# Re-ordered queues in an RWKV-7 recurrence with a SwiGLU feed-forward on one core

## The chip, the cores and the metric

The kernel runs on one core of a Trainium2 chip. The metric is the device time of one launch in microseconds (us). A core has five engines that run side by side, each with a queue of its own that it works off in order: TensorE (PE in the profile, its weight loads PEld), VectorE (DVE), ScalarE (ACT), GpSimd (POOL) and SyncE (SP). SP only issues transfers (DMAs). POOL also issues transfers, and ACT a few at the start. An engine whose next instruction waits for a semaphore holds up all that stand behind it in its queue.

## The reference

`B, H, S, D` are 4, 8, 768 and 40. First comes a recurrence over the tokens, for 32 sequences with a 40x40 state each, then a feed-forward over 3072 tokens with a model width of 320 and a hidden width of 1536:

```python
for t in range(S):
    y[:, :, t] = einsum('bhd,bhde->bhe', r[t], state)
    Sa = einsum('bhde,bhe->bhd', state, a[t])
    state = state * w[t][:, :, None, :] - einsum('bhd,bhe->bhde', Sa, b[t]) + einsum('bhd,bhe->bhde', v[t], k[t])
x = y.transpose(0, 2, 1, 3).reshape(B * S, H * D)
xn = x / sqrt(mean(x * x, -1) + 1e-6) * rms_g
out = (silu(xn @ w_gate) * (xn @ w_val)) @ w_out          # all float32
```

## The kernel before, in words

The recurrence is cut into 24 chunks of 32 tokens. A chunk `c` goes through three stages.

- `front(c)` (lines 652 to 758) loads the inputs of the chunk, turns them with TensorE (`turned`, tiles `wan`, `kbn`), and multiplies up the decays level by level (tiles `T`, `A`, `Ab`, `K`, `KN`). At each level TensorE forms products (`gramk`, `ps<-Ab,K` in the profile), VectorE picks parts of them out of PSUM into the triangular matrix `LT` (COPY_PREDICATED, `where`), and ScalarE copies others (`KN<-ps`, `K<-K`). At its end `LT` goes by DRAM (`sB`) into a layout for the inversion, tile `M`.
- `inverse(c)` (lines 760 to 776) inverts that matrix on VectorE with 31 pairs of dependent steps, `tmp<-Yi,M` and `Yi<-Yi,tmp`, and sends the result by DRAM (`sY`) back into `LT`. For the first four chunks `early_inverse(c)` (lines 778 to 806) does half of it on VectorE within `M` and the rest with small matmuls on TensorE (`ps<-M,LT`, `ps<-M`).
- `main(c)` (lines 810 to 937) carries the state: `ps<-ST,aP` and `ps<-VU,LT` give the right-hand side `Xs`, `ps<-Xs,LT` (early: `ps<-Xs,M`) solves it, copies put the solution into `VU` (line 830), `ps<-VU,KN` updates the state `ST`. Then come scores, masked by VectorE and ScalarE into `As` (lines 864 to 876), the level products `ps<-As,KN` summed on VectorE into `y`, the turn of `y`, the norm (`ss`, `x`), and `xg`, the turned input of the feed-forward.

After each pair of chunks `feed(g)` (lines 939 to 970) runs the feed-forward of 256 tokens: for 12 slices of the hidden width the matmuls `ps<-xg,wf` (kinds `h64` and `h`), a SiLU on ScalarE (`sg`, line 962), a product on VectorE (`hT`), and `po<-wf,hT` into the accumulator `po`. The weights of a slice are loaded from DRAM tensors `sW` into one of five buffers `wf`. The tensors `sW` are made once, during the first third, by `narrow` (lines 973 to 991): it loads raw weights into a `wf` buffer, reworks them in three ScalarE and three VectorE steps (`ex`), and stores them.

None of this is issued in the order in which it is written. The helpers (`tt`, `copy`, `act`, `dma`, `pe` and so on, lines 442 to 495) only record pieces. A piece is one instruction, or one group of matmuls of TensorE. `Plan.issue` (lines 322 to 350) then emits the 6028 pieces in the order of the string `ORDER` (lines 33 to 226): each number is a piece, counted from the first piece not yet issued, and each `-` is a filler, a matmul of the identity with itself into an unused part of `po` (line 1015, `po<-ident` in the profile; two instructions), which gives TensorE something to do. So `ORDER` fixes the queue of every engine. The second string, `PAIRS` (lines 228 to 234), tells for each of the 499 uses of PSUM which of three two-bank tiles (`ps0` to `ps2`) it takes; a use can only begin when the one before it on that tile has been read.

Of the kernel before, what the change touches and what calls it, by code (L numbers as in the profile page):

```python
# [33 lines left out]
85 84 76 83 58 78 73 86 74 59 60 75 5 89 61 88 53 77 80 4 43 6 201 7 87 90 44 8 334 62 9 - - - - - - - - 93 10 18 79  # L34
11 12 214 557 13 213 567 14 15 94 566 210 16 17 95 558 108 200 - - - 97 96 19 335 20 21 2 209 22 23 98 25 199 568 26
100 578 202 24 101 107 569 111 57 - - - - - 102 106 124 589 27 122 112 392 109 103 52 119 113 104 54 577 155 125 110
204 105 120 - - - - - - 114 203 117 121 559 211 598 118 46 131 129 132 45 562 560 212 597 563 588 561 394 123 115 136
586 384 133 134 - - - - - 126 130 116 47 564 3 145 383 135 336 128 137 48 144 143 141 587 219 142 51 570 127 565 146
138 337 55 573 1005 216 579 281 393 220 582 608 571 390 234 379 239 607 572 583 580 380 251 574 222 38 221 609 575 581
42 - - - - - - - - 223 82 226 339 91 64 227 338 39 81 139 224 263 576 238 153 56 249 247 590 206 584 228 382 237 591  # L40
272 593 40 233 232 585 381 154 148 594 33 140 205 229 592 389 235 250 28 248 - - 325 236 32 245 36 230 147 260 282 391
246 259 150 35 34 326 595 0 36 270 155 214 148 242 243 62 605 598 230 - 239 40 616 599 601 628 64 49 91 600 602 30 48
626 1135 28 257 603 29 241 68 150 255 65 0 1347 194 0 194 84 173 0 - - - 182 540 200 0 557 184 1 186 935 542 540 0 506
515 527 257 513 300 0 111 97 110 61 112 96 51 439 458 122 50 243 480 0 244 0 58 255 242 0 259 709 104 120 246 708 247
456 470 258 488 719 0 256 470 457 242 0 716 265 487 104 0 268 0 0 265 473 0 262 277 0 273 0 236 0 260 0 269 0 461 241
- - - - - - - 237 242 0 0 278 242 243 252 0 252 0 0 89 0 99 246 0 97 0 230 94 440 0 230 94 440 231 - - - - - - - - -
240 441 244 0 0 468 440 451 255 0 42 468 269 469 258 215 440 239 204 0 0 257 253 203 93 449 92 212 0 235 - - - - - - -
- 246 0 437 0 262 0 246 247 436 245 464 470 258 259 469 260 244 - - 255 471 465 468 466 0 215 466 269 256 445 697 255
478 686 93 94 264 95 687 270 96 266 97 0 97 470 695 2 98 99 3 100 471 101 473 1 102 0 468 99 470 100 471 101 441 102
103 258 104 105 260 106 - - - - - - - - - - - 0 504 106 107 473 108 0 108 502 0 108 109 469 110 111 0 0 0 0 0 - - 13 0  # L50
374 16 146 143 14 147 142 15 13 355 - - - 25 386 358 0 358 386 388 16 387 389 25 390 79 17 391 28 70 147 355 191 69
356 80 148 149 26 359 0 28 2 29 149 0 149 150 29 0 149 31 185 391 23 32 390 29 150 356 151 186 33 389 0 151 29 387 152
27 40 187 153 154 155 156 33 157 158 159 160 161 34 162 36 163 164 37 165 41 391 38 42 392 39 394 561 166 395 393 552
0 42 548 395 209 0 560 165 42 395 548 210 43 428 211 427 557 44 - - - 565 166 558 45 167 549 168 0 566 168 739 565 567
738 571 169 579 - - 45 728 572 0 124 139 0 535 682 0 535 545 140 578 536 141 0 547 545 546 543 578 0 558 554 567 0 519
- - - - - - 517 377 696 378 380 381 695 518 120 685 135 526 - - - - - - 522 686 379 527 382 136 530 383 554 529 121 -
- 141 540 123 523 565 539 122 537 142 125 538 124 524 - - - - 145 525 148 534 149 152 154 551 535 147 555 - - 157 146
# [3 lines left out]
607 367 478 34 568 - - 35 830 594 36 567 820 38 - 476 37 571 366 570 0 605 356 433 434 435 436 120 437 0 317 318 319  # L61
320 441 321 322 323 324 355 456 458 459 442 4 357 325 457 326 327 328 443 0 443 328 329 330 331 357 0 35 331 3 0 37
450 359 3 36 358 331 332 357 333 356 0 462 448 330 461 464 331 332 468 364 447 463 31 467 476 458 333 365 334 335 0
425 439 441 302 426 436 0 6 439 2 0 435 332 2 436 443 444 0 448 332 442 334 443 333 340 449 0 297 329 342 32 330 - 3
33 341 334 0 332 331 0 332 293 441 295 333 0 438 0 436 333 336 295 337 309 438 338 1 375 342 310 365 374 515 27 292 0
362 292 26 28 44 339 29 34 27 32 338 0 646 29 34 336 647 32 0 439 64 315 647 339 440 634 441 63 340 0 287 413 606 312
313 607 623 12 314 615 414 0 410 310 411 603 619 27 412 475 413 620 414 415 621 416 311 633 28 417 812 418 312 625 - -
- - 476 313 419 420 421 822 258 314 422 423 0 810 423 625 637 477 2 0 819 2 257 0 420 421 645 310 422 0 - - - - - 310
422 3 313 32 630 311 423 33 643 424 641 631 312 0 0 637 20 635 420 647 613 21 421 611 648 819 23 38 22 422 809 423 39
659 24 3 612 36 818 424 651 25 808 621 425 59 660 426 249 427 58 0 427 3 25 428 249 4 28 47 0 - 614 428 429 28 430 431  # L70
0 26 25 614 617 484 31 27 627 0 458 590 400 600 401 0 12 582 32 401 33 583 25 0 579 30 21 - - - - - - - - - 588 29 591
22 453 397 428 398 605 23 0 23 429 24 609 0 590 24 397 588 602 1 604 398 601 429 430 399 2 427 0 584 - - - - - - - - -
- - - - - 4 397 0 25 397 4 0 393 394 28 21 23 27 395 598 24 22 424 607 0 35 395 37 396 24 2 424 47 397 398 38 399 400
# [4 lines left out]
976 716 416 663 729 634 977 562 563 717 713 986 665 564 565 566 975 567 401 568 714 569 985 570 571 967 572 723 722 -  # L78
0 403 726 402 572 401 573 0 726 738 736 573 739 574 664 575 737 576 577 3 723 751 578 579 760 580 747 581 582 633 583
4 584 0 584 585 634 586 636 587 635 588 734 633 0 746 588 - - - - - 403 757 589 722 590 3 404 591 592 593 594 595 596  # L80
# [967 lines left out]
```

## Time and profile before

| | us |
|---|---|
| median of 3 runs | 1081.09 (1074.34, 1081.09, 1081.99) |
| the profiled execution's own time | 1082.16 |
| span of the profiled execution, first to last instruction | 1080.3 |
| TensorE busy in it | 1023.1 (95%) |
| VectorE busy | 850.2 (79%) |
| ScalarE busy | 470.6 (44%) |
| POOL busy | 309.5 (29%) |
| mean granted clock of TensorE | 0.967 |

A row of the timeline reads: start, duration, engine, line, operation, output<-inputs, form, count, and in brackets the idle time of the engine just before it with what ended that. Rows that carry line 444 (VectorE), 467, 464 or 470 (ScalarE), 483 (all transfers) and 486 or 489 (TensorE) are those of a helper, so the tiles tell what they are. `<-issue` stands for a wait that ends on nothing that the profile shows. The end of a matmul is modelled. A row of the windows gives for a stretch the busy time and instructions of TensorE, its weight loads, VectorE, ScalarE and POOL, then the granted clock as a share of full speed, the busy share of the transfer engines and GB/s.

### The profile page before, as it was taken

Reading aid. Unit: us, or ns where it says so; the run is one execution under the profiler, and the core shown is the slowest. Engines: PE = TensorE matmul, PEld = TensorE weight load, DVE = VectorE, ACT = ScalarE, POOL = GpSimd, SP = SyncE. Lnnn points to the kernel's source line nnn. Section 1 sums busy time; section 2 is a strip of 40 time slices with the busy share of each in tenths; the row PEclk is TensorE's granted clock in tenths of the full one; section 3 lists DMA queues with packets and bytes.
Section 4 is the critical chain, followed back from the end, with each engine's and each line's share of the span. In section 5 each row is a group of like instructions: output and inputs, shape, how many; then the busy total and the mean of one; then the engine's idle time right before and its main releaser. Section 6 shows DMA issues by size and latency. Waiting matters only on the chain.

```text
span 1080.3 us, 53530 instructions
## 1 busy us (share of the span) xinstructions
PE 1023.1 (95%) x23406; PEld 840.3 (78%) x23406; DVE 850.2 (79%) x2861; ACT 470.6 (44%) x1043; POOL 309.5 (29%) x554
## 2 busy tenths in 40 slices
PE   6878899999999999999999999999999999999998
PEld 6767777877888777787778778778777887887876
DVE  7877768966868988888898789979879889797321
ACT  6846755743443434433434334434425334432211
POOL 9714504130532141341332231331322321210000
PEclk9677989999999999999999999999979999999999
DMA  9965428775564483664465555564636555444252
GB/s 179 206 149 121 73 67 217 227 151 158 126 153 122 105 170 90 152 124 129 123 148 119 129 144 113 126 137 131 153 71 145 123 129 144 121 116 113 79 151 75
DMA packets 172458, 143.35 MB, mean 133 GB/s; under 512 B 125504, under 2 KB 143872, under 8 KB 172224
## 3 DMA queue, kind: packets, MB, share of 16 engines
q1 hardware_dynamic: 153856, 116.96, 42.4%
q0 software_dynamic: 16192, 22.64, 11.9%
q8 instruction: 184, 3.01, 1.2%
q10 hardware_dynamic: 2176, 0.33, 0.3%
q14 instruction: 50, 0.41, 0.1%
HBM read 123.86 MB, written 15.99 MB: 129 GB/s over the span
## 4 chain that ended last, share of the span: by engine, by line
PE 73%; DVE 13%; DMA 5%; ACT 4%; issue 3%; SPq 1%; POOL 0%; ACTq 0%; DVEq 0%
PE ps L486 50%; PE po L486 12%; PE ps L489 9%; DVE LT L444 2%; DVE tmp L444 2%; DVE y L444 2%; DVE Yi L444 2%; SPq L483 1%; DVE K L444 1%; PE po L1015 1%; DMA LT<-sY 1%; DVE As L444 1%; DMA rn<-in_r_dram 1%; DMA wf<-in_moe_w_gate_dram 1%; DVE hT L444 1%
## 5 line engine op out<-in xcount | busy, mean ns | idle before, releaser
L486 PE MATMUL ps<-xg,wf 128*128 128x256 f32 (+1 forms) x1728 | 358.6, 395 | 4.2 <-DVE xg L444 1.9
L486 PEld LDWEIGHTS ps<-xg,wf 128*128 128x128 f32 (+1 forms) x1728 | 263.9, 191 | 61.6 <-issue 15.9
L486 PE MATMUL po<-wf,hT 128*128 128x320 f32 x576 | 179.9, 445 | 1.8 <-issue 1.3
L464 ACT ACTIVATE sg<-ps 128x256 f32<-128x256 f32 x144 | 53.5, 383 | 239.0 <-PE ps L486 236.4
L444 DVE TENSOR_TENSOR tmp<-Yi,M 128x60 f32<-128x60 f32 (+24 forms) x620 | 130.1, 210 | 17.1 <-DMA M<-sB 2.7
L444 DVE TENSOR_TENSOR Yi<-Yi,tmp 128x60 f32<-128x60 f32 (+24 forms) x620 | 129.8, 209 | 13.9
L483 POOL DMA_DIRECT2D VU<-in_v_dram x92 | 53.2, 584 | 285.9 <-PE ps L486 149.0
L486 PEld LDWEIGHTS po<-wf,hT 128*128 128x128 f32 x576 | 102.0, 189 | 37.3 <-issue 3.7
L444 DVE TENSOR_TENSOR hT<-ps,sg 128x256 f32<-128x256 f32 x144 | 59.5, 420 | 67.5 <-ACT sg L464 66.2
L444 DVE TENSOR_TENSOR K<-K,T 128x512 f32<-128x512 f32 (+1 forms) x192 | 93.9, 499 | 11.7 <-PE ps L486 5.4
L486 PEld LDWEIGHTS ps<-Ab,K 40*64 40x64 f32 x4608 | 78.9, 139 | 30.0 <-issue 10.5
L486 PE MATMUL ps<-Ab,K 40*64 40x56 f32 x4608 | 89.1, 226 | 11.2 <-issue 2.4
L467 ACT COPY K<-K 128x256 f32<-128x256 f32 (+1 forms) x168 | 71.3, 442 | 60.5 <-PE ps L486 42.8
L444 DVE TENSOR_TENSOR As<-ps,msi 128x256 f32<-128x256 f32 (+1 forms) x186 | 78.4, 475 | 15.8 <-PE ps L486 15.0
L467 ACT COPY KN<-ps 128x640 f32<-128x640 f32 x96 | 66.1, 690 | 54.2 <-PE ps L489 22.1
L483 POOL DMA_DIRECT2D kbn<-in_b_dram x92 | 53.5, 585 | 112.6 <-PE ps L486 112.0
L486 PEld LDWEIGHTS ps<-As,KN 128*40 128x40 f32 x3072 | 65.7, 124 | 14.9 <-issue 9.1
L486 PE MATMUL ps<-As,KN 128*40 128x32 f32 x3072 | 72.8, 204 | 1.5 <-issue 1.0
L483 POOL DMA_DIRECT2D kbn<-in_k_dram x92 | 53.5, 585 | 69.6 <-PE ps L486 69.6
L483 POOL DMA_DIRECT2D wn<-in_w_dram x92 | 51.3, 564 | 72.7 <-DVE KN L444 23.6
L444 DVE TENSOR_TENSOR y<-y,ps 128x256 f32<-128x256 f32 x119 | 49.9, 420 | 18.9 <-PE ps L486 16.3
L1015 PE MATMUL po<-ident 128*128 128x128 f32 x302 | 49.8, 319 | 6.6 <-DVE po L517 3.3
(133 smaller groups left out, 1560.4 us busy)
## 6 DMA issues: line engine op xcount, KB each, us to landing
wf<-sW SPq DMA_DIRECT2D x144, 480.0 KB, 4.2
M<-sB SPq DMA_DIRECT2D x80, 128.0 KB, 3.6
rn<-in_r_dram SPq DMA_DIRECT2D x24, 160.0 KB, 4.8
sW<-ex SPq DMA_DIRECT2D x16, 240.0 KB, 4.1
out_dram<-o SPq DMA_DIRECT2D x48, 80.0 KB, 4.2
kbn<-in_k_dram POOLq DMA_DIRECT2D x92, 40.0 KB, 3.8
kbn<-in_b_dram POOLq DMA_DIRECT2D x92, 40.0 KB, 3.6
wan<-in_a_dram POOLq DMA_DIRECT2D x46, 80.0 KB, 4.7
```

The lines of the kernel that those rows point to most:

```text
L444: plan.add("DVE", kind, lambda at: fn(at(o), *m(at)), [o], aps(*args))
L464: plan.add("ACT", "act", lambda at: nc.scalar.activation(at(o), at(a), f, **kw), [o] + aps(acc), [a])
L467: plan.add("ACT", "copy", lambda at: nc.scalar.copy(at(o), at(a)), [o], [a])
L483: plan.add(by, "dma", lambda at: queue.dma_start(out=o, in_=i), [o], [i])
L486: return o, lhsT, rhs, lambda at: nc.tensor.matmul(at(o), lhsT, rhs, start=start, stop=stop, skip_group_check=True)
L489: return o, i, ident, lambda at: nc.tensor.transpose(at(o), i, ident)
L1015: plan.warm = lambda: nc.tensor.matmul(po_[:, 0, DM:DM + P], ident, ident, start=False, stop=False, skip_group_check=True)
```

## The change

Only the two strings change. All 6028 pieces and all 151 fillers are issued in both kernels, and each piece is the same instruction. Counted by engine, the fewest pieces that have to be taken out and put elsewhere to turn the old queue into the new one are 12 of 905 on TensorE (the last at 342 us of the profile before), 26 of 1024 on ScalarE, 111 of 2858 on VectorE, 31 of 545 on POOL and 55 of 696 on SP. No piece moves by more than 9 places in its queue (2 on TensorE, 6 on ScalarE, 7 on VectorE and POOL, 9 on SP). 306 of the 499 digits of `PAIRS` differ, and fillers move from one gap of TensorE to another within the first 240 us.

The start of the diff:

```diff
-85 84 76 83 58 78 73 86 74 59 60 75 5 89 61 88 53 77 80 4 43 6 201 7 87 90 44 8 334 62 9 - - - - - - - - 93 10 18 79
-11 12 214 557 13 213 567 14 15 94 566 210 16 17 95 558 108 200 - - - 97 96 19 335 20 21 2 209 22 23 98 25 199 568 26
+85 84 76 83 58 78 73 86 74 59 60 75 5 89 61 88 53 77 80 4 43 6 201 7 87 90 44 8 334 62 9 - - - - - - - - 93 10 18 11
+12 214 13 213 567 557 79 14 15 94 566 210 16 17 95 558 108 200 - - - 97 96 19 335 20 21 2 209 22 23 98 25 199 568 26
...
```

Read as queues, with the start that each piece has in the profile before (the piece is named by its stage, chunk or slice), the places of which the prediction speaks are these. A minus is the old order, a plus the new one.

```diff
 TensorE, queue
-226.67 main(4) ps<-VU,LT   227.39 main(4) ps<-rE,Sd   228.15 front(6) ps<-ident,kbn   229.06 main(3) ps<-ident,x   filler   230.32 feed(0) h64   231.39 h (first)   233.22 h (second)
+228.15 front(6) ps<-ident,kbn   226.67 main(4) ps<-VU,LT   227.39 main(4) ps<-rE,Sd   230.32 feed(0) h64   233.22 h (second)   229.06 main(3) ps<-ident,x   231.39 h (first)
 TensorE, fillers ahead of a piece
-front(3) ps<-ident,K at 128.98: 0    main(2) ps<-ST,aP at 135.58: 1    main(0) ps<-Xs,M at 78.44: 2
+front(3) ps<-ident,K at 128.98: 2    main(2) ps<-ST,aP at 135.58: 2    main(0) ps<-Xs,M at 78.44: 0
 ScalarE
-178.61 narrow ex<-ex   179.12 main(2) x<-x
+179.12 main(2) x<-x   178.61 narrow ex<-ex
-195.22 Ab<-Ab   195.42 ex<-ex   196.02 KN<-ps   196.70 K<-K   197.12 VU<-ps x3   198.42 ex<-ex   199.14 ex<-wf
+195.42 ex<-ex   196.02 KN<-ps   197.12 VU<-ps x3   198.42 ex<-ex   195.22 Ab<-Ab   199.14 ex<-wf   196.70 K<-K
-809.79 o<-po   810.38 Yi<-eye   810.69 Sd<-ps   811.27 main(17) x<-ps,ss
+811.27 main(17) x<-ps,ss   809.79 o<-po   810.38 Yi<-eye   810.69 Sd<-ps
-834.37 K<-K   834.67 KN<-ps   835.26 sg<-ps   835.53 y<-ps   836.63 KN<-ps
+834.67 KN<-ps   835.26 sg<-ps   835.53 y<-ps   836.63 KN<-ps   834.37 K<-K
 VectorE
-365.38 tmp<-Yi,M   365.51 feed(2) hT<-ps,sg
+365.51 feed(2) hT<-ps,sg   (three others)   365.38 tmp<-Yi,M
-645.41 Yi<-Yi,tmp   645.53 main(13) xg<-ps,gcol
+645.53 main(13) xg<-ps,gcol   645.41 Yi<-Yi,tmp
-691.39 LT<-near,ps   (seven others)   693.90 main(14) xg<-ps,gcol
+693.90 main(14) xg<-ps,gcol   691.39 LT<-near,ps   (seven others)
-739.36 tmp<-Yi,M   739.63 Yi<-Yi,tmp   739.90 main(16) VU<-ps
+739.90 main(16) VU<-ps   739.36 tmp<-Yi,M   739.63 Yi<-Yi,tmp
-944.65 tmp<-Yi,M   944.90 main(21) VU<-ps
+944.90 main(21) VU<-ps   944.65 tmp<-Yi,M
-116.29 main(1) As   116.62 As   116.95 As
+116.62 As   116.95 As   116.29 main(1) As
 POOL
-67.54 wn   68.09 wn   68.64 wn   70.15 M<- (inverse 0)   70.70 wn   82.08 M<- (inverse 2)
+70.15 M<- (inverse 0)   82.08 M<- (inverse 2)   68.64 wn   67.54 wn   68.09 wn   (four others)   70.70 wn
 SP
-78.61 wf<-sW   81.75 M<-sB   82.11 M<-sB
+81.75 M<-sB   82.11 M<-sB   78.61 wf<-sW
```

More of the change, by code (lines that the diff above doesn't have):

```diff
@@ L39 @@
[L39 to L53, printed above, removed]
@@ L62 @@
[L62 to L71, printed above, removed]
@@ new lines @@
+42 - - - - - 223 226 339 91 64 227 338 39 81 238 139 224 263 576 153 56 249 247 590 206 584 228 382 237 591 272 593 40
+233 232 585 381 154 148 594 33 140 229 592 389 235 250 28 205 248 - - 325 236 32 245 36 230 147 260 282 391 246 259
+150 35 34 326 595 0 36 270 155 214 148 242 243 62 605 598 230 - - - - 239 40 616 599 601 628 64 49 91 600 602 30 48
+626 1135 28 257 603 29 241 68 150 255 65 1413 260 261 151 240 67 - - - 251 609 269 69 66 627 254 71 256 1005 612 610
+70 604 0 515 527 257 513 300 0 111 97 110 61 112 96 51 458 122 50 243 461 480 0 244 0 58 255 242 0 259 709 104 120 246
@@ new lines @@
+708 247 470 258 719 0 256 105 470 455 488 435 487 242 266 0 0 268 0 0 265 473 0 262 277 0 273 0 236 0 260 0 269 0 461
+241 - - - - - - - 237 242 0 0 278 242 0 242 251 252 0 0 89 0 99 246 0 97 0 230 94 440 0 230 94 440 0 230 - - - - - - -
+- - 239 440 243 0 255 468 451 0 42 439 468 269 469 258 215 695 440 239 204 0 0 257 203 93 449 92 212 0 0 234 - - - - -
+- - - 245 437 0 250 262 0 246 247 436 245 464 470 258 259 469 260 244 - - 255 471 465 468 466 0 466 - - 269 256 445
+215 255 478 93 94 264 95 270 96 266 97 0 97 470 2 98 99 3 100 471 101 473 1 102 0 468 99 470 100 471 101 441 102 103
@@ new lines @@
+474 258 104 105 260 106 - - - - - - - - - - - 0 106 107 108 0 108 0 108 109 469 501 502 110 111 0 0 0 0 0 13 0 16 146
+562 572 561 143 14 147 142 374 15 13 355 - - - 25 386 358 0 358 386 388 16 387 389 25 390 17 391 28 147 355 191 69 79
+80 570 356 148 149 150 359 0 69 28 2 29 359 0 149 150 29 151 33 187 24 393 25 34 392 31 152 153 188 35 391 154 32 390
+0 0 152 27 40 187 153 154 155 156 33 157 158 159 160 161 34 162 36 163 164 37 165 41 391 38 42 392 39 394 559 561 166
+395 393 552 0 42 548 395 209 0 549 548 560 42 165 395 210 43 428 44 211 427 - - - 565 166 558 45 167 168 0 168 739 565
@@ new lines @@
+567 566 571 169 579 45 572 0 124 139 0 535 682 691 0 535 141 545 140 578 536 0 547 545 546 555 543 578 0 558 567 520 -
+- - - - - 518 378 697 0 378 380 381 695 518 120 685 677 135 526 - - - - - - 522 686 379 527 382 136 530 383 554 529
+121 - - 141 540 123 565 539 537 523 142 125 538 124 524 - - - - 145 525 148 534 152 154 149 551 535 147 555 - - 157
+146 550 536 150 155 151 556 165 552 153 564 160 691 164 161 692 0 161 689 162 165 1 0 546 676 0 510 45 558 46 560 47
+424 511 999 0 555 44 996 45 563 509 421 432 508 436 435 422 437 433 571 443 441 434 444 46 572 829 0 572 441 585 838
@@ new lines @@
+625 - - - 476 313 419 420 421 822 258 314 422 423 0 810 423 625 477 2 637 0 257 423 2 424 648 313 0 422 0 - - - - -
+310 422 3 313 32 630 311 423 33 641 643 631 424 312 0 0 637 20 635 420 647 613 21 421 611 648 819 23 38 22 422 809 810
+423 39 659 24 3 612 36 818 424 651 25 808 4 621 425 59 660 426 249 427 58 0 427 25 428 249 4 429 28 0 - 614 429 28 430
+431 0 25 614 26 617 484 31 42 27 627 0 458 400 590 600 401 0 12 582 401 583 25 0 579 29 28 30 27 21 - - - - - - - - -
+588 591 22 397 428 23 398 605 0 23 452 429 24 0 590 24 397 588 602 1 398 601 429 430 2 427 0 605 0 583 395 - - - - - -
```

34 lines of the change are left out of this document (16 added, 18 removed), and 220 rows, old and new, of the table ORDER.

## The prediction

> **What bounds the kernel now.** I read the page first (busy shares, granted clock, chain), then busy time by stretch, then the waits of TensorE one by one in the timeline, and for each the queue of the engine that ended it.
>
> ```profile
> span 1080.3 us, 53530 instructions
> PE 1023.1 (95%) x23406; PEld 840.3 (78%) x23406; DVE 850.2 (79%) x2861; ACT 470.6 (44%) x1043; POOL 309.5 (29%) x554
> PEclk9677989999999999999999999999979999999999
> PE 73%; DVE 13%; DMA 5%; ACT 4%; issue 3%; SPq 1%; POOL 0%; ACTq 0%; DVEq 0%
> ```
> ```profile
> 0.00:200.00 200.00, 168.18 (x4296) 147.35 (x4297) 158.24 (x491) 127.07 (x267) 88.58 (x177) 0.86 0.67 149
> 360.00:1080.30 720.30, 697.46 (x15693) 565.72 (x15692) 567.53 (x1944) 271.46 (x614) 173.98 (x297) 0.99 0.51 124
> ```
>
> Two regimes. In the first 200 us TensorE is busy for 168.18, fillers included, at a clock of 0.86, and VectorE for 158.24: there several queues share the limit. From 360 us on TensorE is busy for 697.46 of 720.30. Its work is not touched there, so moved steps of other engines can win only from the 22.84 us in which it stands, and from its clock. That is the first bound: two thirds of the kernel hold 22.84 us, and a step that nobody waits for brings nothing.
>
> **The change, part by part.** Nothing is added or removed: pieces and fillers are the same in number, so the sum consists only of waits that shrink or grow. A step that goes back by one place is late by one neighbour, 0.2 to 0.8 us; it costs nothing while the step that reads it starts later than that anyway. For most moves that is so, because the queues other than TensorE's are full of work done ahead. I went through the moved steps and kept those where the reader was seen waiting. First third:
>
> ```profile
> 179.43 0.33 PE L489 MATMUL ps<-ident,x 128*128 128x128 f32 x1 [0.84 <-ACT x L467]
> 198.11 0.60 PE L1015 MATMUL po<-ident 128*128 128x128 f32 x4 [0.62 <-issue]
> 230.32 0.49 PE L486 MATMUL ps<-xg,wf 64*128 64x256 f32 x2 [0.55 <-ACT K L467]
> ```
> ```profile
> 178.61 0.63 ACT L464 ACTIVATE ex<-ex 128x480 int32<-128x480 int32 x1
> 179.12 0.25 ACT L467 COPY x<-x 128x64 f32<-128x64 f32 x1
> ...
> 195.22 0.29 ACT L467 COPY Ab<-Ab 128x128 f32<-128x128 f32 x1
> ...
> 196.70 0.40 ACT L467 COPY K<-K 128x256 f32<-128x256 f32 x1
> 197.12 1.28 ACT L467 COPY VU<-ps 32x320 f32<-32x320 f32 x3
> ```
>
> - At 179.43 TensorE stood 0.84 us for the copy x<-x, which the new queue puts ahead of the 0.63 us step ex<-ex. Its start moves from 179.12 to 178.61: -0.5. The step that goes back feeds the weight preparation, whose next instruction is late by 0.25.
> - The three copies into VU at 197.12 now run ahead of Ab (0.29) and K (0.40); TensorE's next weights wait behind the last of them and behind fillers, and the idle time shown there is 0.62. Two copies of 0.69 together cover it: -0.6. The fillers stay, so no more than the idle time can be won.
> - At 230.32 TensorE waited 0.55 for the copy of K that follows the turn of kbn. The new queue has that turn two groups earlier, so the wait goes: -0.55. Two groups behind it finish one turn later; what they feed is the solution that next holds TensorE at 237, with VectorE and ScalarE steps between, so I give this back in the losses below.
>
> Together -1.65. Then the bulk transfers:
>
> ```profile
> 81.11 0.82 PE L486 MATMUL ps<-Xs,M 32*32 32x40 f32 x34 [1.92 <-issue]
> 75.12 0.57 PE L486 MATMUL ps<-M,LT 16*16 16x16 f32 x39 [3.38 <-DMA M<-sY]
> 78.61 0.49 SPq L483 DMA_DIRECT2D wf<-sW  x1
> 67.54 1.67 POOL L483 DMA_DIRECT2D wn<-in_w_dram  x3 [4.84 <-DVE KN L444]
> ```
> ```profile
> M<-sY SPq DMA_DIRECT2D x4, 24.0 KB, 3.2
> ```
>
> At 81.11 the group that solves chunk 0 stopped halfway for 1.92 us, with no semaphore to show for it, while a 480 KB weight load issued at 78.61 was under way; the new queue puts that load behind the two M<-sB transfers of 81.75. At 75.12 TensorE waited 3.38 for the M<-sY loads, whose 3.2 us to landing overlap four wn loads from POOL; the new queue puts those behind the two memsets. What the load costs others is not seen in a row, so I bound it: 0 (stops put down to issue also occur where no such load runs) to -1.92 for the first, and 0 to -0.9 for the second (3.2 against the 2.3 of the quickest sY transfer in that stretch). I take -1.0 and -0.4, about the middle of each, as nothing decides between the ends. The loads themselves come later by some 5 and 14 us and are read tens of us later: nothing.
>
> The rest, where TensorE's order stands:
>
> ```profile
> 365.98 0.55 PE L489 MATMUL ps<-ident,x 128*128 128x128 f32 x3 [0.68 <-DVE hT L444]
> 646.14 0.49 PE L486 MATMUL ps<-xg,wf 64*128 64x256 f32 x2 [1.00 <-DVE xg L444]
> 692.94 0.49 PE L486 MATMUL ps<-xg,wf 64*128 64x256 f32 x2 [0.28 <-DVE LT L444]
> 740.53 0.51 PE L489 MATMUL ps<-ident,VU 128*104 128x128 f32 x3 [0.47 <-DVE tmp L444]
> 811.43 0.40 PE L489 MATMUL ps<-ident,K 104*128 104x104 f32 x2 [0.25 <-ACT Sd L467]
> 814.65 0.49 PE L486 MATMUL ps<-xg,wf 64*128 64x256 f32 x2 [0.20 <-ACT Ab L467]
> 835.41 0.40 PE L486 MATMUL ps<-Ab,K 40*64 40x56 f32 x12 [0.83 <-ACT KN L467]
> 945.53 0.36 PE L486 MATMUL ps<-VU,KN 64*40 64x40 f32 x17 [0.27 <-DVE Yi L444]
> ```
> ```profile
> 739.36 0.24 DVE L444 TENSOR_TENSOR tmp<-Yi,M 128x75 f32<-128x75 f32 x1
> 739.63 0.24 DVE L444 TENSOR_TENSOR Yi<-Yi,tmp 128x75 f32<-128x75 f32 x1
> ```
> ```profile
> 834.05 0.71 ACT L467 COPY K<-K 128x256 f32<-128x256 f32 x2 [2.35 <-PE ps L486]
> ```
>
> Before each of these a step that TensorE reads goes ahead of others. At 740.53 a VU copy passes the two inversion steps of 739.36 and 739.63 (0.48 in all, the wait is 0.47): -0.47. At 692.94 xg passes seven steps and at 811.43 the norm's x three copies, which is more than the waits of 0.28 and 0.25: both go, and with the second the 0.20 at 814.65, which hangs on the same x. At 646.14, 945.53 and 365.98 one inversion step is passed: about -0.24, -0.24 and, as the step is shorter there and overlaps, -0.14. At 835.41 the copy KN that ends the wait passes one of the two copies K<-K: half of 0.71, less their overlap, -0.31. Sum: 0.47 + 0.28 + 0.25 + 0.20 + 0.24 + 0.24 + 0.14 + 0.31 = 2.13. The larger waits stay (0.5 of 0.83, 0.76 of 1.00), since another input is late next.
>
> Against this stand steps that go back in front of a waiting reader. In the first third: an As product at 116.29 behind two others, about 0.3 beyond TensorE's start on it, and the two groups at 227 late by one turn. In the rest: an LT piece at 532.74 behind a K product, some 0.2, and two such of 0.1 to 0.2. I put all of them at +1.0, between 0 (covered) and +2.
>
> Moved POOL loads of single chunks (kbn, wn, VU) change places with loads of the same chunk; all of a group are needed before the turn that reads them, so the order among them gives nothing. The 306 other PSUM digits mostly rename tiles in step, and the first use of each waits for the same kind of reader: 0.
>
> Sum: -1.65 - 1.0 - 0.4 - 2.13 + 1.0 = -4.2 us. The profiled execution took 1082.16, 1.07 above the median of 1081.09, so it becomes 1078.0 and, against the median, 1076.9.
>
> **The clock.** One resource is left out of that sum.
>
> ```profile
> 124.00:136.00 12.00, 8.88 (x358) 7.62 (x351) 8.73 (x23) 9.53 (x25) 8.72 (x15) 0.99 0.73 106
> 136.00:146.00 10.00, 10.00 (x187) 8.08 (x181) 6.39 (x25) 3.53 (x6) 0.00 (x0) 0.50 0.06 11
> 788.00:801.00 13.00, 13.00 (x216) 10.34 (x213) 8.22 (x25) 3.02 (x6) 2.31 (x4) 0.50 0.23 41
> ```
> ```profile
> 135.58 0.86 PE L486 MATMUL ps<-ST,aP 40*32 40x40 f32 x64 [1.31 <-DVE K L444]
> 784.93 0.28 PE L486 MATMUL ps<-Ab,K 40*64 40x56 f32 x4 [1.44 <-DVE LT L444]
> ```
>
> Twice a stretch in which TensorE is busy throughout ran at a clock of 0.50: 10 us from 136 and 13 us from 788. At full clock that work takes half, so they cost up to 5.0 and 6.5 us. Each follows a cluster of short waits (1.31 at 135.58, 1.44 at 784.93). The spread of the runs shown, 1081.09 against 1074.34, is 6.75, the size of one such stretch. The change puts two fillers and one more filler into the gaps just ahead of 136 (two fillers take 0.60, the row at 198.11), which may keep the first stretch at full clock; at 785 nothing is done for the wait. I leave both stretches in the sum, since no row shows how much filling is enough, and put them in the range.
>
> [...]
>
> **The rivals.**
>
> 1. The halved stretches go: -4.2 and up to -11.5, so 1065 to 1072. For it: the fillers put ahead of 136, and the fastest run shown. Against: the wait of 1.44 at 784.93 stays, and a stretch may come up elsewhere.
> 2. Slower: the inversion is starved. Its 62 dependent steps per chunk are what many moved steps pass on VectorE, and its result reaches TensorE by two transfers.
>
> ```profile
> 490.73 0.36 PE L486 MATMUL ps<-Xs,LT 32*32 32x40 f32 x17 [0.68 <-DMA LT<-sY]
> ```
> ```profile
> 483.52 7.17 DMA LT<-sY
> ```
>
> At 490.73 TensorE already waits for LT, so in some chunks there is no slack. If each of the 20 late inversions came 0.8 us late (one KN or three inversion steps) with no slack, that is +16, less the 4.2: about 1093. It decides from a mean lateness beyond slack of 0.8 us. Against it: steps of an inversion go back by at most 5 places and the others close up behind, and this row is the only such wait of this length after 360 us; the transfers of LT at 480 go forward in the new SP queue.
> 3. The change does nothing that counts: every shortened wait is replaced by the next input, or by a wait that the profile puts down to issue. Then 1080 to 1082.
>
> **How the numbers follow.** The forecast, a small gain from waits (1074 to 1079): 0.37. Rival 1: 0.34. Rival 2: 0.14. Rival 3: 0.15. A difference of 1% (10.8 us) is about what a measurement of this kernel can tell from no change. Below 1070.3 lies most of rival 1, and a part of the forecast's case where the bulk loads bring their upper bound: faster 0.34. Above 1091.9 lies rival 2 past its deciding point, with one more halved stretch: slower 0.13. The rest, 0.53, is within 1%. The range leaves out the far ends: 1063 is the forecast with both stretches gone and the transfers at their bound (1076.9 - 11.5 - 1.4 = 1064.0, with 1 us to spare); 1088 is the forecast with losses at +2 and rival 2 at half its price or a halved stretch more (1076.9 + 1 + 8 = 1085.9, with 2 to spare).
>
> **What would show it.** In the changed profile the waits listed above are gone or shorter: no 0.47 ahead of ps<-ident,VU of chunk 16, no 0.55 ahead of h64 of feed(0) at about 230, the stop inside ps<-Xs,M of chunk 0 shorter than 1.92. TensorE's idle time after 360 us falls from 22.8 to about 20. The granted clock shows whether the slice after 136 and the one after 788 are still at half. If TensorE's idle time after 360 us does not fall, the sum is wrong in its second part; if it falls and the time does not, the clock or the first 200 us took it back. A wait for DMA LT<-sY in many chunks would show rival 2.

## The result and the profile after

Over 20 runs each, the changed kernel takes 1073.96 us in the median (1071.04 to 1078.18), the kernel before 1080.29 (1071.76 to 1091.65). The ratio is 0.9952 with a 95% interval of 0.9934 to 0.9969, a gain of 3.3 to 7.1 us. The profiled execution of the changed kernel took 1075.73.

The page of the changed kernel, in the lines that answer to those shown of before:

```profile
span 1074.0 us, 53529 instructions
PE 1017.0 (95%) x23406; PEld 836.4 (78%) x23406; DVE 844.3 (79%) x2861; ACT 470.1 (44%) x1043; POOL 310.8 (29%) x554
PEclk8877989989999999999999999999999999999999
PE 78%; DVE 11%; issue 4%; ACT 3%; POOL 2%; DMA 2%; SPq 0%; DVEq 0%; ACTq 0%; POOLq 0%
```

Its busy time by stretch (TensorE, its weight loads, VectorE, ScalarE, POOL, granted clock, transfers):

```profile
0.00:200.00 200.00, 167.82 (x4297) 146.55 (x4298) 157.78 (x494) 127.73 (x268) 89.92 (x177) 0.87 0.67 150
200.00:360.00 160.00, 155.29 (x3393) 124.66 (x3391) 119.14 (x407) 68.47 (x156) 43.87 (x75) 0.98 0.57 144
360.00:1074.00 714.00, 693.89 (x15719) 565.14 (x15718) 567.36 (x1962) 273.95 (x620) 177.00 (x302) 1.00 0.52 126
```

TensorE's idle time after 360 us is 714.00 - 693.89 = 20.11, against 22.84 before, and the slice at half clock in the last third is gone from the clock row. But idle time is counted against the clock on the wall, and the two kernels are not at the same place at 360 us. The better reading takes one and the same step in both traces. One group of products of feed(2) starts at 358.75 before and at 363.18 after: 4.4 us late. A group of feed(7), later on, is early. Before:

```profile
777.71 0.97 PE L486 MATMUL po<-wf,hT 128*128 128x320 f32 x3
```

After:

```profile
775.97 0.97 PE L486 MATMUL po<-wf,hT 128*128 128x320 f32 x3
```

So in this pair of profiles the first third lost 4.4 us and the stretch from there to 778 us gained 6.2 (from 4.4 late to 1.7 early, before rounding). The last gain is the stretch at half clock:

```profile
785.00:798.00 13.00, 11.40 (x418) 9.71 (x406) 10.86 (x32) 4.19 (x8) 3.05 (x6) 1.00 0.37 86
```

The same work now runs at a clock of 1.00 (0.50 before), which brought 4.6 us by the next steps. One execution each is little; the experiments give more of them.

Waits of TensorE in the changed kernel, at the places for which the prediction has a term:

```profile
72.28 0.79 PE L486 MATMUL ps<-M,LT 16*16 16x16 f32 x64 [1.22 <-DVE M L444]
77.48 0.87 PE L486 MATMUL ps<-Xs,M 32*32 32x40 f32 x34 [2.30 <-issue]
177.01 0.33 PE L489 MATMUL ps<-ident,x 128*128 128x128 f32 x1 [0.44 <-ACT x L467]
197.85 0.72 PE L1015 MATMUL po<-ident 128*128 128x128 f32 x5 [1.12 <-issue]
233.81 3.06 PE L486 MATMUL ps<-xg,wf 64*128 64x256 f32 x16
370.13 0.55 PE L489 MATMUL ps<-ident,x 128*128 128x128 f32 x3 [0.40 <-DVE hT L444]
645.71 1.13 PE L486 MATMUL ps<-xg,wf 64*128 64x256 f32 x8 [0.87 <-DVE xg L444]
738.57 1.08 PE L489 MATMUL ps<-ident,VU 128*104 128x128 f32 x8
806.42 0.49 PE L489 MATMUL ps<-ident,x 128*128 128x128 f32 x3
828.36 1.15 PE L486 MATMUL ps<-Ab,K 40*64 40x56 f32 x64 [0.72 <-ACT KN L467]
939.33 0.81 PE L486 MATMUL ps<-VU,KN 64*40 64x40 f32 x64
```

A row without brackets has no wait left; none is left at 692.94 and 814.65 either. (The profile of one of the experiments, "named", is of its slowest run, 1087.82 us against 1071.19 to 1086.42 for its others, and stays out of the means below.) The terms of the rest add up nearly as forecast, and yet most of the gain is not in them, as the next sections show.

### The profile page after: what moved, and what is told of

Same layout as the page of the kernel before. It is cut to its first block, busy times and chain, and to the rows that moved or that the text cites. A ratio compares the mean times of both kernels' runs of the same rounds, so it can differ in the third digit from the quotient of the medians.

```text
span 1074.0 us, 53529 instructions
## 1 busy us (share of the span) xinstructions
PE 1017.0 (95%) x23406; PEld 836.4 (78%) x23406; DVE 844.3 (79%) x2861; ACT 470.1 (44%) x1043; POOL 310.8 (29%) x554
## 3 DMA queue, kind: packets, MB, share of 16 engines
q8 instruction: 184, 3.01, 1.2%
## 4 chain that ended last, share of the span: by engine, by line
PE 78%; DVE 11%; issue 4%; ACT 3%; POOL 2%; DMA 2%; SPq 0%; DVEq 0%; ACTq 0%; POOLq 0%
PE ps L486 53%; PE po L486 14%; PE ps L489 10%; PE po L1015 1%; DVE LT L444 1%; DVE As L444 1%; DVE tmp L444 1%; DVE K L444 1%; DVE y L444 1%; DVE Yi L444 1%; POOL kbn L483 1%; DVE hT L444 1%; ACT KN L467 1%; DVE wf L444 0%; ACT K L467 0%
## 5 line engine op out<-in xcount | busy, mean ns | idle before, releaser
L444 DVE TENSOR_TENSOR As<-ps,msi 128x256 f32<-128x256 f32 (+1 forms) x186 | 78.5, 477 | 13.7 <-PE ps L486 12.7
L444 DVE COPY_PREDICATED LT<-near,ps 128x384 f32<-128x384 uint32 (+2 forms) x72 | 52.2, 726 | 1.9 <-DMA out_dram<-o 0.8
```

What stands on the lines that cost most here:

```text
L444: plan.add("DVE", kind, lambda at: fn(at(o), *m(at)), [o], aps(*args))
```

## The experiments

All kernels compute the whole reference; only the two strings differ. "Old" and "new" stand for the queues of the kernel before and of the changed kernel. Ratios are to the kernel before, run on the same chip beside each of them.

**1 to 4: which part of the change brings what.** The cut is put where both kernels have issued the same pieces, with TensorE at about 350 us. "First" and "rest" take along the PSUM digits of their part (87 and 219 of the 306), the other two keep the old ones.

```diff
 first:       -old up to 350 us  +new up to 350 us;  old behind
 rest:         old up to 350 us;  -old behind  +new behind
 rest_dve:     as before, behind 350 us +VectorE's new queue alone
 rest_other:   as before, behind 350 us +the new queues of ScalarE, POOL and SP alone
```

> Queues of the changed kernel up to TensorE's step at about 350 us, those of the kernel before behind it. Theory A (the sum on record: waits -1.65, transfers -1.4, losses up to +1.0 in the first third): about 2 us faster than before, 0.998. Theory B (read off the two profiles: TensorE reaches 345 us 4.9 us later in the changed kernel, by a stop of 2.69 us at 214 and a stretch at half clock behind it, both caused by the new order): 3 to 5 us slower, 1.004. Theory C (that stop and the half-clock stretches come by chance): 0 to 2 us faster, and no stop over 2 us at 214 in its profile.

Measured: 1083.64 us, ratio 1.0031 (0.9999 to 1.0064).

> Queues of the kernel before up to about 350 us, those of the changed kernel behind it. Theory A: 2.1 us faster, 0.998. Theory B: the many short waits of TensorE that went between 390 and 800 us (7 us by the profiles) and the half-clock stretch at 788 (4.4 us) belong to the order: 7 to 11 us faster, 0.990 to 0.993, and no half clock at 788. Theory C: the waits go as in the changed kernel but the stretch at 788 comes by chance: 5 to 7 us faster.

Measured: 1073.45 us, ratio 0.9941 (0.9914 to 0.9968). The profile shows no half clock at 788.

> The kernel before, with the moved steps of VectorE alone behind about 350 us; the other queues and the PSUM tiles as before. Theory A (xg, VU and hT ahead of inversion steps): 1.5 of the 2.1 us, all but the terms of ScalarE. Theory B: two thirds of the gain of the rest, 4 to 6 us. If the gain of the rest comes from the transfers that SP issues earlier (the inversion's results), this one is the same as before within 1 us.

Measured: 1075.32 us, ratio 0.9960 (0.9931 to 0.9989).

> The kernel before, with the moved steps of ScalarE, POOL and SP alone behind about 350 us; VectorE's queue as before. Theory A: 0.6 to 0.8 us faster (the norm's x at 811, KN at 835). Theory B: 1 to 3 us faster, among it the wait of 0.68 for LT<-sY at 490. If the gain comes from VectorE alone, the same as before.

Measured: 1080.26 us, ratio 0.9993 (0.9964 to 1.0022).

Theory A, 2 us in either part, falls; B has both signs right, although the 6.4 us of "rest" lie in the 5 to 7 of its theory C and below the 7 to 11 of B. The whole gain, and more, lies behind 350 us: 6.4 us (3.5 to 9.3). The moves of the first third cost 3.3 us (-0.1 to +6.9) where a gain was forecast. Of the rest, VectorE's moves alone bring 4.3 (1.2 to 7.5); those of the other engines are not told from nothing. The PSUM digits were not tested alone, and 4.3 and 6.4 are not told apart, so what the digits bring stays open.

**5 and 6: a stop near 214 us.** In the two profiles with the new first third (the changed kernel and "first") TensorE stops in the level products of main(3), for 2.69 and 1.67 us. In the four with the old one (before and kernels 2 to 4) it is 0.06 to 0.41. After and, in the second fence, before:

```profile
213.95 0.26 PE L486 MATMUL ps<-As,kbn 128*40 128x32 f32 x2
216.90 0.35 PE L486 MATMUL ps<-As,kbn 128*40 128x32 f32 x5 [2.69 <-issue]
```
```profile
214.20 1.09 PE L486 MATMUL ps<-As,kbn 128*40 128x32 f32 x32
```

All inputs of these products had been written by 211.5, so no data are late. On SP two weight loads (480 KB each) now follow one another. After, then before:

```profile
209.37 0.86 SPq L483 DMA_DIRECT2D wf<-sW  x2
210.29 1.10 SPq L483 DMA_DIRECT2D sB<-LT  x2
```
```profile
209.13 0.37 SPq L483 DMA_DIRECT2D wf<-sW  x1
210.16 0.32 SPq L483 DMA_DIRECT2D sB<-LT  x1
210.53 0.44 SPq L483 DMA_DIRECT2D wf<-sW  x1
```

The profile lists what could be late: instructions come by DMA too, on queue q8 in packets of 16 KB (3.01 MB in 184), at the pace at which TensorE runs through its own (233 to 275 a packet, see the last section). The page of before has this row, and for the changed kernel the transfers between 214.5 and 215.6 us have the second (none is in the window from 209 to 214.5, in which the transfer engines are busy for a share of 0.94):

```profile
q8 instruction: 184, 3.01, 1.2%
```
```profile
q8 instruction: 1, 0.02, 5.4%
```

That packet lands at 215.52, and TensorE goes on at 216.90. In the profile before it came between 212 and 213.2, ahead of the need. Two kernels move this one load:

```diff
 pair (from before), SP
-wf<-sW (slice 55)  sB<-LT  wf<-sW (slice 44)  sB<-LT
+wf<-sW (slice 55)  wf<-sW (slice 44)  sB<-LT  sB<-LT
 apart (from the changed kernel), SP
-wf<-sW (slice 55)  wf<-sW (slice 44)  sB<-LT  sB<-LT
+wf<-sW (slice 55)  sB<-LT  wf<-sW (slice 44)  sB<-LT
```

> The kernel before with one step moved: on SP the second of two 480 KB weight loads near 210 us (slice 44 of feed(0)) goes ahead of the sB<-LT transfer that stood between them, as in the changed kernel. Theory (instructions late): TensorE's own instructions arrive in packets of 16 KB by the same transfer engines, and two weight loads back to back hold such a packet up; then TensorE stops in the level products near 214 us for 1.5 to 2.7 us (0.06 to 0.41 in the four profiles with the old order there), about 1.3 us after such a packet lands, and often a stretch at half clock follows: 2 to 5 us slower, 1.002 to 1.005. Rival (the stop comes from other moves of the first third, or by chance): a stop below 0.5 us, and the same time as before.

Measured: 1083.60 us, ratio 1.0033 (1.0003 to 1.0063). Its profile has the stop:

```profile
209.99 0.26 PE L486 MATMUL ps<-As,kbn 128*40 128x32 f32 x3
212.16 1.01 PE L486 MATMUL ps<-As,kbn 128*40 128x32 f32 x29 [1.91 <-issue]
```

> The changed kernel with that one step put back: the sB<-LT transfer between the two 480 KB loads. Theory (instructions late): the stop near 214 us falls from 2.69 us to below 0.5 and no half clock follows at 216; 2 to 5 us faster than the changed kernel, 0.990 to 0.993 of the time before. Rival: the stop stays at 1.5 or more, and the time stays at 0.995.

Measured: 1073.15 us, ratio 0.9933 (0.9904 to 0.9961). The stop shrinks, and no half clock follows:

```profile
208.56 0.77 PE L486 MATMUL ps<-As,kbn 128*40 128x32 f32 x30 [0.47 <-issue]
```

One load one place ahead costs 3.6 us (0.3 to 6.8), as the theory had it. Taking it back is in the right direction (0.9933 against 0.9952), but the two intervals overlap, so the time alone doesn't settle it. TensorE's place supports it: between two steps at 202 and 239 us it falls back by 4.0 us in the changed kernel and 3.3 in "pair", and by 0.3 in "apart". In "first", with a stop of 1.67 but no half clock behind it, it is 0.8, no more than in the profiles with the old queue there (0 to 1.4). The control is not perfect: the stop is 0.00, 0.19, 0.29, 0.79 and 0.80 in the other later profiles that have the old queue there, and 1.38 in that of "named".

**7: the first 120 us.**

```diff
 head: +new up to 120 us;  old from 120 to 350 us;  +new behind 350 us
```

Two fillers are lost at the seams (149 are left), and its PSUM digits are those of neither kernel (298 differ from before, 276 from the changed kernel).

> Queues of the changed kernel up to 120 us and from 350 us on, those of the kernel before between. In its first part the wait for M<-sY is 0.9 to 1.2 us in place of 3.3 to 4.0, and TensorE was some 4 us ahead at 120 us in both profiles with that part. Theory A (a lead at 120 us is kept): 0.990 to 0.991, 3 to 4 us faster than the kernel with the moves behind 350 us alone (0.994). Theory B (between 120 and 200 us another queue sets the pace, and the lead is used up there): 0.994, the same as that kernel.

Measured: 1070.98 us, ratio 0.9910 (0.9883 to 0.9938), the fastest of all. It has the new first 120 us without the pair of loads at 210. This is theory A's number; but the interval overlaps that of "rest" (0.9914 to 0.9968), and in its profile TensorE is only 1.3 us ahead at 120 us, so that the lead is kept is likely, not shown. It is faster than the kernel before; its interval and that of the changed kernel (0.9934 to 0.9969) overlap slightly, so that it beats that one too is likely, not shown.

**8: the moves that the sum had counted.**

```diff
 named: as before, behind 350 us only
+VectorE: hT 365.51, xg 645.53, xg 693.90, VU 739.90, VU 944.90 ahead, as listed in the change
+ScalarE: x 811.27 and KN 834.67 ahead, as listed in the change
```

> The kernel before with only those blocks of moved steps behind 350 us that the sum on record counts: hT at 365, xg at 645 and 693, VU at 740 and 945 on VectorE, x at 811 and KN at 834 on ScalarE. If the sum's list is complete: 2.1 us faster, 0.998, and nearly all of the gain of the kernel with all moves behind 350 us (0.994) would then have another cause. If the list was too short: 1.5 to 2.5 us faster too, and the waits at 413, 454, 490, 501, 534 and 613 stay as before in its profile (0.37, 0.52, 0.75, 0.77, 0.47, 0.47), which go in that kernel.

Measured: 1080.55 us, ratio 0.9991 (0.9956 to 1.0025): 1.0 us faster, between 4.8 faster and 2.7 slower. The forecast of 2.1 for these lies within, but the 6.4 us of all moves behind 350 us does not. One of the seven turned against itself: with xg ahead, TensorE waits for a piece of LT that went back instead, 0.72 where it was 0.28.

```profile
697.43 0.49 PE L486 MATMUL ps<-xg,wf 64*128 64x256 f32 x2 [0.72 <-DVE LT L444]
```

In the kernel with all moves behind 350 us that wait is gone. Three waits that the sum had not counted, and that go there (the last down to 0.18), stay in "named", at 0.38, 0.47 and 0.47. In the profile before they are:

```profile
413.44 0.75 PE L486 MATMUL ps<-Ab,K 40*64 40x56 f32 x36 [0.37 <-DVE tmp L444]
533.87 1.16 PE L486 MATMUL ps<-Ab,K 40*64 40x56 f32 x64 [0.47 <-DVE K L444]
613.48 0.73 PE L486 MATMUL ps<-Ab,K 40*64 40x56 f32 x34 [0.47 <-DVE LT L444]
```

Of the other three that were named ahead of the run, the one at 490 is gone here too; those at 454 and 501 are put down to issue, and stand at neighbouring products here, at 1.09 and 0.71.

**9 to 11: what brings the early lead, and the half clock at 788.**

```diff
 memset (from before), POOL
-wn  wn  wn  M<- (inverse 0)  wn
+M<- (inverse 0)  wn  wn  wn  wn
 dma120: as before, up to 120 us +the new queues of SP and POOL alone
 gap785: as before, +the new queues of all engines between 755 and 800 us alone
```

> The kernel before with one step moved: on POOL the memset of M (inverse of chunk 0, at 70.15 in the profile before) goes ahead of the three wn loads issued from 67.54. The M<-sY transfers, which SP issues right behind that memset, then start 1.5 us earlier. Theory (this move is the early gain): the wait of 3.3 to 4.0 us for M<-sY near 75 falls to 1 to 2 us, and TensorE keeps it: 2 to 3 us faster, 0.997 to 0.998. Rival (the gain needs the other moves of the first 120 us, or is used up before 200 us): the wait falls, and the time stays within 1 us of before.

Measured: 1079.46 us, ratio 1.0020 (0.9985 to 1.0054). The theory fell: its 0.997 to 0.998 lie outside, and the wait is 2.92 in place of 3.38, not 1 to 2. The memset runs at 69.85 (70.15 before), since it waits for another transfer, which the first row names:

```profile
69.85 0.21 POOL L479 MEMSET M<- 128x128 f32 x1 [6.93 <-DMA sY<-M]
```
```profile
74.78 0.90 PE L486 MATMUL ps<-M,LT 16*16 16x16 f32 x64 [2.92 <-DVE M L444]
```

That transfer stands on SP, at 67.75 before and 65.28 in the changed kernel. The three wn loads had not held the memset up. What they cost the M<-sY loads was not tested here, since all four are now issued beside them (M<-sY from 70.34), where the changed kernel issues them 10 us later. Here, then there:

```profile
70.43 2.26 POOL L483 DMA_DIRECT2D wn<-in_w_dram  x4 [0.37 <-DVE tmp L444]
```
```profile
79.04 1.67 POOL L483 DMA_DIRECT2D wn<-in_w_dram  x3 [0.27 <-issue]
```

> The kernel before with the moved steps of SP and POOL alone up to 120 us. Theory: the whole lead of the changed kernel at 120 us (some 4 us in three profiles) comes from these transfers: 3 to 4 us faster, 0.996 to 0.997. Rival: fillers and the steps of VectorE and ScalarE bring half of it or more: 0 to 2 us faster.

Measured: 1076.28 us, ratio 0.9970 (0.9937 to 1.0002). That is the theory's number, but the interval reaches 1. In its profile TensorE is 4.4 us ahead at 120 us and 6.2 at 239. The profiles (see the table below) bear the theory out: at 120 us the six with the new order of SP and POOL lead by 1.3 to 5.0 us, 3.3 in the mean, and the two with that order alone (this one and "dmarest") by 4.4 and 2.1; the eight with the old one lie between 3.3 ahead and 2.2 behind, in the mean 0.2 behind. One place shows how: the M<-sY loads near 70 us land after 1.9 to 2.3 us in those four of the six where it can be read, and after 2.6 to 3.7 in the others. But the six also have less half clock up to there, 37 us in the mean against 44, so part of the lead may be the clock's.

> The kernel before with the changed order of all engines between 755 and 800 us alone: on VectorE the pieces of LT that TensorE waits for at 784.93 go ahead of a K product, on SP some loads change places. Theory A (the waits cause the half clock there): the wait of 1.44 us before the products of front(19) goes, no half clock near 788 in the profile (it is there in 4 of the 6 profiles with the old order, for 3.4 to 13.7 us, and in none of the 4 with the new), and on average 2.5 us less are lost: 0.997 to 0.998. Theory B (the half clock comes by chance): the wait goes, the time is the same within 1 us, and half clock near 788 is as likely as before. The statement on record, that nothing is done there for this wait, would have it stay at 1.44.

Measured: 1078.98 us, ratio 0.9991 (0.9961 to 1.0021). The time is the same within the interval. The wait of 1.44 goes, another comes, and the clock holds:

```profile
786.00 0.76 PE L486 MATMUL ps<-Xs,LT 32*32 32x40 f32 x58 [1.11 <-DMA LT<-sY]
```
```profile
788.00:801.00 13.00, 11.37 (x431) 9.64 (x432) 11.22 (x35) 4.93 (x10) 2.31 (x4) 1.00 0.34 75
```

**12: both gains together.**

```diff
 dmarest: +new queues of SP and POOL up to 120 us;  old from there to 350 us;  +new behind 350 us
```

> The kernel before with the changed queues of SP and POOL alone up to 120 us, and of all engines behind 350 us. If the gains add up (0.997 for the first part, 0.994 for the second, each by its own run): 0.991, 9 to 10 us faster than before, and as fast as the kernel that takes all queues of the changed kernel up to 120 us (0.991): then neither the fillers nor the moved steps of VectorE and ScalarE in the first 120 us are needed. If these are needed, or the early lead is used up: 0.994, as with the moves behind 350 us alone.

Measured: 1073.61 us, ratio 0.9933 (0.9905 to 0.9960), between the two expectations; it doesn't tell them apart.

## Where TensorE stood

Each number is the start of one and the same TensorE step in that kernel's trace, less its start in the trace of before, in us (minus is earlier). The columns are the steps that start before at 120.13, 238.70, 358.75 and 778.52; then the gain from the third to the fourth, and the sum of TensorE's waits between these two.

| kernel | 120 | 239 | 359 | 779 | 359 to 779 | waits there |
|---|---|---|---|---|---|---|
| before | 0 | 0 | 0 | 0 | 0 | 12.2 |
| first | -5.0 | -1.0 | -1.1 | +1.2 | +2.3 | 14.3 |
| pair | -1.4 | -0.9 | -0.1 | +1.5 | +1.6 | 13.7 |
| memset | +2.2 | 0.0 | +0.7 | +2.9 | +2.1 | 14.0 |
| dma120 | -4.4 | -6.2 | -5.9 | -2.1 | +3.8 | 14.1 |
| gap785 | +1.9 | +0.6 | 0.0 | +3.2 | +3.2 | 13.9 |
| named | 0.0 | +2.8 | +3.1 | +4.7 | +1.5 | 13.9 |
| rest_dve | +1.2 | +1.1 | +1.3 | -0.4 | -1.7 | 11.7 |
| rest_other | -3.3 | -1.3 | -0.7 | +2.6 | +3.2 | 14.4 |
| changed | -3.7 | +3.8 | +4.4 | -1.7 | -6.2 | 8.2 |
| rest | +1.1 | -0.5 | -0.9 | -6.4 | -5.6 | 9.0 |
| apart | -3.3 | -6.0 | -5.7 | -9.9 | -4.2 | 10.0 |
| head | -1.3 | -5.0 | -4.4 | -5.9 | -1.4 | 11.1 |
| dmarest | -2.1 | -1.3 | -0.9 | -4.0 | -3.1 | 10.8 |

- Between 359 and 779 the six profiles with the old queues (before, first, pair, memset, dma120, and gap785, which is new from 755 us only) lie at 0 to +3.8, mean +2.2; the five with the new ones at -6.2 to -1.4, mean -4.1. The difference of 6.3 us is about the gain that "rest" shows in time (6.4). The profile of before was a good draw: it is the lowest of its six. Behind 779 us the moves bring little: where the half clock at 788 does not come, TensorE gains 4.2 to 4.4 us on before up to 1070 us with the old queues (first, memset, dma120) and 3.5 to 5.7 with the new.
- Their waits are 13.7 and 9.8 in the mean. So 3.9 us of the 6.3 are waits that went; the other 2.4 are products that take less time in the profile, 406.0 us against 408.4 (half clock accounts for 0.2 of that). Where a wait goes TensorE can gain a little more than its length (0.54 us for the 0.47 at 533.87), which does not account for the 2.4; it stays open.
- At 239 apart, head and dma120 lead by 5.0 to 6.2 us; dmarest leads by 1.3, no more than old queues do. The kernels with the two loads side by side in the new first third are at -1.0 (first) and +3.8 (changed). Chance is in this column. Before, changed, first, rest_other, dmarest and named have half clock for 6.8 to 10.2 us from some point between 133 and 137 us on. The others have none there, and gain 4.2 to 5.3 us on before by it. Rest, rest_dve, pair, memset and gap785 have lost that again at 239 (-0.9 to +1.1); apart, head and dma120 keep the most of it.
- First and changed have lost 3.2 and 3.5 us of their lead by 202 us. The half clock from 134 on doesn't explain that, since before has it too; what does stays open. The changed kernel then loses 4.0 at the stop.

## Why the prediction was right, and where it was wrong

The forecast was 1076.9, a gain of 4.2 us; measured are 3.3 to 7.1, mostly from waits of TensorE behind 350 us. Sign, size and kind are right; the size is so by luck, since its parts are not.

- **First third, -1.65.** Two of three terms happened: 0.84 became 0.44 at the turn of x (-0.4 for -0.5), and the wait of 0.55 for K is gone. The third failed in its reason. The 0.62 before the fillers at 198.11 was laid to the copies into VU; the fillers read nothing new, and 0.62 became 1.12. A packet of TensorE's instructions lands 1.4 us before the end of the wait in both profiles (196.75 and 196.48), as at the stop of 214: it is instructions that are late there.
- **Bulk transfers, -1.4.** The stop of 1.92 at 81.11 was laid to a weight load under way, -1.0. The load was moved and the stop is 2.30; with the old queues it is 0.56 to 2.40. Here too a packet of instructions lands 1.3 us before the end, in both profiles (79.84 and 76.15). The 0.4 at 75.12 was mis-sized, its reason holds as far as seen: with the wn loads behind both memsets the M<-sY loads land in 1.9 to 2.3 us, not 2.6 to 3.7, and from the first of their issues to TensorE's step it takes 3.3 to 3.4 us in the six profiles with the new order of SP and POOL, 3.4 to 4.7 (mean 4.4) in the others. That is 1.0 us, about its bound of 0.9. SP's order changes with it, so the wn loads alone are not shown to do it. The wait, 3.38 before and 1.22 after, is no measure of it, as it depends on when TensorE comes. In "dma120" the step starts 3.3 us earlier than before, and the wait is still there:

```profile
71.84 0.77 PE L486 MATMUL ps<-M,LT 16*16 16x16 f32 x64 [3.54 <-DVE M L444]
```

- **What the first third lost.** The +1.0 for losses named an As product and two groups at 227. The loss is elsewhere, and larger: one of the 55 moved steps on SP puts two loads side by side, which I had passed over since both are read tens of us later. That is true of the loads. What they hold up is a third party, the instructions of TensorE (the packet that lands at 215.52, 1.4 us before the stop of 2.69 ends), and no queue in the diff shows those.
- **The rest, -2.13.** In this pair of profiles the eight terms came to 0.28 + 0.13 + 0.28 + 0.47 + 0.25 + 0.20 + 0.11 + 0.27 = 1.99, but single ones were off (0.14, 0.24 and 0.31 were forecast for the first, second and seventh). The 0.11 at 835.41 is no gain: the wait there is 0.00 to 0.84 in the profiles with the old queues and 0.69 to 0.73 in the five with the new. The step that failed is the one ahead of the sum, the choice of waits: it left out two thirds of the gain. A part of this was to be seen beforehand: the waits at 413.44, 533.87 and 613.48 end on a VectorE step that the row names, and they went (the last down to 0.18). The first two are gone with VectorE's moves alone; the third is at 0.48 with these and at 0.18 with those of the other engines alone.

  The prediction has a further reason in its third rival, that a wait shortened on one input goes over to the next input. It used it against the gain only. It works the other way too: where several inputs are advanced together, a wait goes that no single move shortens. The one at 692.94 is 0.24 to 0.28 with the old queues, 0.72 in "named", 0.48 with VectorE's moves alone, 0.24 with the others alone, and gone in all five kernels with both (these have the new PSUM digits too, to which the sum gave 0). How much of the gain is of this kind is not shown. Some may be the clock's: (1 - granted clock) x span, half the time at half clock, is 23.6 us in the mean of the 11 runs of "rest" (2.0 either way at 95%) and 26.3 (1.4 either way) in the 34 runs of before beside it.
- **The clock.** The fillers ahead of 136 were to keep the first stretch at full clock. In the changed kernel they did not; they stood still themselves, and the half clock came as before:

```profile
133.89 0.64 PE L1015 MATMUL po<-ident 128*128 128x128 f32 x3 [1.70 <-issue]
```
```profile
134.00:144.00 10.00, 10.00 (x216) 8.04 (x216) 5.43 (x24) 3.53 (x6) 0.36 (x1) 0.50 0.08 14
```

  With the same fillers it came in "first" (6.8 us) and not in "apart"; with the old ones it came in 4 of 11 profiles. So it comes and goes either way, and what the fillers do for it is not shown.

  "At 785 nothing is done for the wait" was wrong: pieces of LT go ahead of a K product there, and the 1.44 is gone. Whether the half clock at 788 goes with it stays open. It is there in 4 of the 7 profiles in which the wait is 1.00 to 1.45 (before, rest_dve and named for 13.7 us, pair for 3.4) and in none of the 7 in which it is 0.39 or nothing. The 1.00 is that of VectorE's moves alone:

```profile
784.09 1.16 PE L485 MATMUL ps<-Ab,K 40*64 40x56 f32 x64 [1.00 <-DVE LT L443]
```

  Where it is long, TensorE gains 0.6 us at most from the step at 778.52 to one at 809.59, against 4.1 to 5.1 elsewhere. But "gap785", which changes only this place, is 1.0 us faster with an interval from 4.2 faster to 2.3 slower.
- **Rival 2, the starved inversion,** did not come: the wait of 0.68 for LT at 490.73 is gone (as in two of the other five with the old queues there). One came up at 781, and it is alone:

```profile
781.05 0.76 PE L486 MATMUL ps<-Xs,LT 32*32 32x40 f32 x58 [1.10 <-DMA LT<-sY]
```

So the sum came out near the truth by luck, since two errors have opposite signs: a first third put down as a gain of 2.05 that cost about 3, and a rest worth three times its term.

## What to carry to other kernels

Compare two traces at the same step of the bounding engine, not by its idle time, and let the kernels that share a part of the order serve as repeats: a single pair of profiles was off by 2 us here in either direction. List every wait of the bounding engine that ends on a named step, and see whether that step, or one ahead of it in its queue, has moved. When steps of several queues feed one reader, cost the moves together, since the wait ends with the last input (the one at 692.94 was 0.48 and 0.24 with either part of the moves, and gone with both). Before moving a bulk load that nobody needs soon, ask what else uses the transfer engines at that moment, the instruction packets of the busiest engine above all, and keep two large loads from standing side by side where that engine runs through many short instructions (here two of 480 KB ahead of 32 products in 1.09 us; one load one place ahead cost 3.6 us, 0.3 to 6.8).

## What the runs showed of the hardware

TensorE's instructions are loaded by DMA as well. In the page of before 184 packets of 16 KB carry 3.01 MB. No row names the engine that they are for, but their pace is TensorE's: between 18.62 and 998.96 us of that trace, cut at the landing of every eighth packet, TensorE starts 1861 to 2199 products and weight loads in a stretch (233 to 275 a packet), whether the stretch takes 36.9 us or 61.2, while VectorE starts 84 to 159. Over the whole span it is 2 x 23,406 = 46,812 in 184 packets, 254 a packet. In the profile before, 24 of the 51 waits of at least 0.3 us that TensorE has after the first 10 us (19.1 of 42.5 us) end 1.1 to 1.8 us after such a packet has landed; with a packet about every 5.8 us, some 6 would by chance. The profile calls many of them "issue", and some it puts down to a semaphore, as the 1.31 at 135.58, which ends 1.3 us after a landing. Fillers are among these instructions: the waits of 0.62 at 198.11 before and of 1.70 at 133.89 in the changed kernel, ahead of fillers that read nothing new, end 1.4 and 1.7 us after a landing.

Half clock followed on one of these stops: in the changed kernel TensorE stops for 2.69 us before 216.90, and the clock is 0.50 from 216.02 to 222.84, so it fell after 1.8 us of the stop. In "first" a stop of 1.67 was not followed by it at that place: the clock is 1.00 from 216 to 223. Over 12 runs of "first", (1 - granted clock) x span is 30.6 us in the mean (2.2 either way at 95%), against 26.3 (1.4 either way) in the 34 runs of the kernel before beside it. That is half the time at half clock, and so the most that it costs, as the same work takes about twice as long there: before, eight products ps<-xg,wf (128x256) take 3.78 us from 797.17, at 0.50, and 1.99 from 804.95, at 1.00. The 4.3 us more could cover the 3.3 us by which "first" is slower, but this is not shown: a mean over runs does not tell where the stretches lie, and "rest_other" has 22.7 of it and is no faster than before.
